# Low value products between the transposes of a head's last run

## The chip, the cores and the metric

The kernel runs on one core of one Trainium2 chip. The metric is the device time of one execution in microseconds (us): before the change the median of 3 runs is 1168.23 us (1168.02 to 1168.42).

## The reference

The program is attention with decay, followed by a feed-forward network (FFN), in float32. Shapes: 8 batches, 8 heads, 576 tokens, 64 dimensions a head; the FFN goes from 512 to 2048 and back for 4608 tokens.

```python
scores = scale * np.matmul(q, k.transpose(0, 1, 3, 2))
decay = cum[:, :, :, None] - cum[:, :, None, :]        # cum: running sum of log f
scores = np.where(causal, -1000000000.0, scores + decay)
attn = np.exp(scores - np.max(scores, axis=-1, keepdims=True))
attn = attn / (np.sum(attn, axis=-1, keepdims=True) + 1e-09)
attn_out = np.matmul(attn, v)
h = x @ w_in                                           # x: the heads side by side
g = np.maximum(h, 0.0) + np.log1p(np.exp(-np.abs(h)))
out = g @ w_out
```

## The kernel before

**Numbers in two halves.** Most products are made of float32 numbers split into a high half in a reduced format (float32r) and a low half, the rest. A product of two such numbers is then a few fast products instead of one slow one. For the values V both halves stand side by side in one stationary tile of 128 columns, `vhl`: columns 0 to 63 are the high half, 64 to 127 the low one. A product with it gives 128 rows of output, and the rows of the two halves are added at the end (`shift` and `put`, L1082 to L1086). The names h and l below are the high and low half of the attention weights.

**A whole head.** 56 of the attention's 70 jobs are whole heads (`whole`, L557); the others, of the first batch, work in plain float32 and are not touched. A whole head goes in these steps. Scores of five query tiles are computed (`stat_tile`, L773), reduced to the row's extreme on VectorE (L804), exponentiated on ScalarE (L832) and scaled by their sums (L862). The weights then lie with queries on partitions, and the value product wants keys there, so they are transposed on TensorE, run by run (`weights`, L872). A run fills one PSUM bank:

- run 0: the small one, 64 queries against the first keys, and the last 64 keys
- run 1: keys 0 to 127, 512 queries, four transposes
- run 2: keys 128 to 255, 448 queries, four transposes
- run 3, the last: keys 256 to 383 with 320 queries and keys 384 to 511 with 192, five transposes

In `turn` (L924) a run takes a bank and transposes its blocks (L927). `hi_part` and `lo_part` (L939, L943) then split the bank into h and l in SBUF (`ph` and `pl`, three buffers each). On the profile's rows the tile of a bank of transposes is `b`, its operands are the weights `p` (stationary) and a constant (`ident`, or `halves`, which also exchanges two halves of 64) as the moving operand of 128 columns.

`output` (L1046) makes the value products of a group of queries in one bank, tile `o`. Group 0 has the first 64 queries, group 1 the other 512. For each key chunk it multiplies `vhl` with h and then with l, over as many moving columns as there are queries: in group 1 these are 512 and 512 for the first chunk, a single one of 64 for the small run, then 448 and 448, 320 and 320, 192 and 192 (L1060).

**The order of the work.** The order on every engine is written down before anything runs. `Plan` (L52) holds operations with an estimated cost, what they come after, and the buffers that they take and give; `run` (L106) always emits the operation that can start earliest by its estimates. Costs are those of `on_pe`, `on_turn` (0.109 us a transpose) and their like (L158 to L188). Operations that need a bank of the tag `att` (four banks, shared by scores, transposes and value products) take it in the order in which they were added, but for scores, which may go ahead where a bank is to spare. On the chip each engine works through its own list in order and waits for the others by semaphores.

A head's runs and outputs are added among the scores of the next head (L1549 to L1562): runs 0 to 2, the output of group 0, run 3, and later the output of group 1. Between these units, parts of the FFN are added, a share of what is ready (`run_ffn`, L1482). So TensorE's list alternates between attention and groups of six FFN products (`up_part`, L1176, with tile `h` at L1210; `products`, L1290, with tile `acc` at L1295). The FFN's work goes on after the last head.

Of the kernel before, what the change touches and what calls it, by code (L numbers as in the profile page):

```python
# [157 lines left out]
def on_pe(n, times=1, m=128):  # L158

    return On("PE", times * (max(n * 0.000444, m * 0.00092) + 0.002))  # L160
# [7 lines left out]
def on_turn(n):  # L168

    return On("PE", 0.109 * n)  # L170
# [49 lines left out]
def tile_decay_attention_softplus_ffn(  # L220
# [51 lines left out]
    def bank(tag, name):  # L272
        return psum.tile([P, 512], F32, tag=tag, name=name, bufs=BUFS[tag])
# [334 lines left out]
    def attention(job):  # L608
# [26 lines left out]
        n = f"{number}"  # L635
# [236 lines left out]
        def weights(bi):  # L872
            spans, w = [], 0
            for key, lo, hi, vi, vc in banks[bi]:
                spans.append((key, lo, hi, (vi, vc), w))
                w += hi - lo


            small = spans[0][:3] == (0, 0, 64)
            blocks, need = [], []  # L880
            for ti, (q0, n_q, k0, pi, po) in enumerate(tiles):
                for key, lo, hi, _, at in spans if small else reversed(spans):
                    if q0 < hi and q0 + n_q > lo and k0 <= key:

                        second = q0 < lo and ti < nt - 1
                        at += q0 - lo + (64 if second else 0)
                        c = po + key - k0
                        if small:  # L890

                            x = pt[pi][:, c : c + 64]
                            one = halves
                            if key == 0:

                                x, one = x[0:68], ident[0:68, 0:68]
                            blocks.append((x, key // 8, one))
                        else:
                            one = halves if second else ident
                            blocks.append((pt[pi][:, c : c + P], at, one))  # L900
                        need += st["norm"][ti]
            box = {}
            sums = job["sums"].get(bi, []) if plain else []
            if sums:
                st["one", bi] = box, w
                need.append(st["over"])
                at1 = w
                w += sum(x[3] for x in sums)

            spread_ = []  # L910
            for ta, tb, *_ in sums:

                def spread(e, ta=ta, tb=tb):
                    one = box["one"] = buf("one", [P, P], f"one{n}_{bi}")
                    x = rs[:, ta : tb + 1]
                    x = bass.AP(x.tensor, x.offset, [x.ap[0], [tb - ta, 2], [0, 64]])
                    copy(e, one.rearrange("p (a b) -> p a b", a=2), x)

                if ta != tb:
                    on = [on_dve(P, True, bias=COPY_BIAS), on_act(P), On("POOL", 0.3)]  # L920
                    spread_.append(add(on, spread, after=[st["over"]], takes=("one",)))
            need += spread_

            def turn(e):  # L924
                box["ps"] = bank("att", f"b{n}_{bi}")
                for x, at, one in blocks:
                    e.transpose(box["ps"][0 : x.shape[1], at : at + one.shape[1]], x, one)  # L927
                for ta, tb, at, _ in sums:
                    one = rs[:, ta : ta + 1].to_broadcast([P, P]) if ta == tb else box["one"]
                    e.transpose(box["ps"][:, at1 + at : at1 + at + P], one, ident)  # L930

            def keep(e):
                box["p"] = buf(tag, [P, 512], f"p{n}_{bi}", F32R)[:, 0:w].bitcast(F32)
                copy(e, box["p"], box["ps"][:, 0:w])

            more, size = ("64", P) if small else ("", 512)
            rows = 64 if small else P

            def hi_part(e):  # L939
                box["h"] = buf("ph" + more, [P, size], f"ph{n}_{bi}", F32R)[:, 0:w]  # L940
                copy(e, box["h"][0:rows], box["ps"][0:rows, 0:w])

            def lo_part(e):  # L943
                if small:
                    h = box["h"]
                    e.tensor_sub(h[64:P], box["ps"][0:64, 0:w], h[0:64].bitcast(F32))
                    return
                box["l"] = buf("pl", [P, size], f"pl{n}_{bi}", F32R)[:, 0:w]
                e.tensor_sub(box["l"], box["ps"][:, 0:w], box["h"].bitcast(F32))  # L949

            need = list(dict.fromkeys(need)) + halves_set
            m = add(on_turn(len(blocks) - 0.48 * small + len(sums)), turn, after=need, takes=("att",))
            for _ in spread_:
                give("one", [m])
            st.setdefault("turned", []).append(m)
            if bi == len(banks) - 1:
                give("p", st["turned"])
                if plain:
                    give("stat", st["turned"])
            on = [on_act(w, psum=True), on_dve(w)]  # L960
            if plain:
                tag = tags[bi] = ("ph", "pl")[count["p"] % 2]
                count["p"] += 1
                ready = [add(on, keep, after=[m], takes=(tag,))]
                give("att", ready)
            else:
                hp = add(on, hi_part, after=[m], takes=("ph" + more,))
                ready = [hp, add(on_dve(w), lo_part, after=[hp], takes=() if small else ("pl",))]
                give("att", ready[1:])
            for key, lo, hi, vc, at in spans:  # L970
                parts.append((lo, hi, bi, vc, at, box, ready, small))
# [74 lines left out]
        def output(gi):  # L1046
            g0, g1, h, tok = groups[gi]
            g, j = h // 2, h % 2
            todo = sorted(
                (p for p in parts if p[0] < g1 and p[1] > g0), key=lambda p: (max(p[0], g0) > g0, p[2])  # L1050
            )
            box, last = {}, []
            for i, (lo, hi, bi, vc, at, pbox, ready, small) in enumerate(todo):
                a, z = max(lo, g0), min(hi, g1)

                def values(e, i=i, a=a, z=z, vc=vc, o=at + a - lo, pbox=pbox, xs="h" if small else "hl"):
                    if i == 0:
                        box["ps"] = bank("att", f"o{n}_{gi}")
                    for x in xs:
                        e.matmul(  # L1060
                            box["ps"][:, a - g0 : z - g0], st["vhl"][:, vc[1], :],
                            pbox[x][:, o : o + z - a],
                            start=i == 0 and x == "h", stop=i == len(todo) - 1 and x == xs[-1],
                        )

                on = on_pe(z - a, len("h" if small else "hl"))
                op = add(
                    on, values, after=ready + last + st["V"],
                    takes=("att",) if i == 0 else (),
                )  # L1070
                last = [op]
                used[bi].append(op)
            st.setdefault("ends", []).extend(last)
            w = g1 - g0


            def to():
                if b not in x_of:
                    x_of[b] = buf("x32", [P, NCC, S], f"x32_{b}")
                return x_of[b][64 * j : 64 * j + 64, g, tok : tok + w]  # L1080

            def shift(e):  # L1082
                copy(e, to(), box["ps"][64 - 64 * j : 128 - 64 * j, 0:w])

            def put(e):
                e.tensor_add(to(), box["ps"][64 * j : 64 * j + 64, 0:w], to())  # L1086

            needs = last + x_taken.get(b, [])
            takes = () if b in x_taken else ("x32",)
            c = add(on_act(w, psum=True), shift, after=needs, takes=takes)  # L1090
            d = add(on_dve(w), put, after=[c])
            x_taken.setdefault(b, [c])
            puts = [d]
            wrote.setdefault(b, []).append((tok, tok + w, d))
            give("att", puts)
            if gi == len(groups) - 1:
                give("T", st["scores"])
                give("vhl", st["ends"])
                for bi, ops in used.items():
                    if banks[bi][0][:3] == (0, 0, 64):  # L1100
                        give("ph64", ops)
                    else:
                        give("ph", ops)
                        give("pl", ops)
# [523 lines left out]
```

## Time and profile before

| | |
|---|---|
| median of 3 runs | 1168.23 us |
| the profiled execution | 1169.16 us |
| its span, first to last instruction | 1167.4 us |
| TensorE products, busy | 1153.1 us (99%) |
| TensorE weight loads, busy | 958.0 us (82%) |
| VectorE, ScalarE, GpSimd, busy | 799.1, 834.1, 146.1 us |
| granted TensorE clock | 1.00 |

In the rows, PE stands for the products of TensorE and PEld for the loads of its stationary operand, which run beside products; DVE is VectorE, ACT ScalarE and POOL GpSimd. A row of a group names line, engine, operation, output and inputs, the stationary operand's rows and columns (128*64 has 64 columns), the shape of the moving operand, and the count; behind the first bar stand busy time in us and the mean of one in ns, behind the second the idle time before them. A row of the timeline has start and covered time in us, and neighbours of the same kind are merged with a count. Products overlap in their pipeline: one takes far longer from its start to its end than from its start to that of the next.

### The profile page before, as it was taken

The page shows a single profiled execution, that of the slowest core. Times are in us where ns is not written, and L with a number is a line of the kernel's source. Part 1 is how long each engine was busy: PE and PEld are TensorE (multiplying, and loading weights), DVE is VectorE, ACT ScalarE, POOL GpSimd, SP SyncE. Part 2 cuts the span into 40 slices and gives each one's busy share as a digit, 9 for nine tenths or more (in the row PEclk, how much of TensorE's full clock was granted, in tenths as well). Part 3 has the DMA queues.
Part 4 walks back from the last instruction along what each step waited for, and adds up shares of the span by engine and source line. Part 5 has one row for each costly group of instructions (what it writes and reads, how often), then busy time and mean ns, then how long its engine had stood idle before and what let it go on. Part 6 is the DMA issues. An engine that isn't in the chain of part 4 may idle for free.

```text
span 1167.4 us, 19457 instructions
## 1 busy us (share of the span) xinstructions
PE 1153.1 (99%) x6236; PEld 958.0 (82%) x6236; DVE 799.1 (68%) x1986; ACT 834.1 (71%) x1987; POOL 146.1 (13%) x158
## 2 busy tenths in 40 slices
PE   8999999999999999999999999999999999999998
PEld 6776788888888888888888888888888888888887
DVE  7889999877776778667877777677866772223322
ACT  6887788978867877678767786787867873444543
POOL 3424221100111101011011001110011100000000
PEclk9999999999999999999999999999999999999999
DMA  8867776555666546656566557654666433211211
GB/s 240 245 211 212 193 187 164 144 153 164 160 195 183 155 133 199 180 156 170 152 173 185 161 152 202 175 153 141 188 169 185 121 110 124 75 54 37 90 55 37
DMA packets 118758, 180.36 MB, mean 155 GB/s; under 512 B 20784, under 2 KB 78416, under 8 KB 118656
## 3 DMA queue, kind: packets, MB, share of 16 engines
q1 hardware_dynamic: 118488, 178.97, 53.7%
q8 instruction: 50, 0.82, 0.3%
q14 instruction: 52, 0.43, 0.1%
q10 hardware_dynamic: 168, 0.15, 0.0%
HBM read 109.98 MB, written 35.95 MB: 125 GB/s over the span
## 4 chain that ended last, share of the span: by engine, by line
PE 85%; DVE 8%; DMA 3%; ACT 2%; issue 1%; SPq 0%; POOL 0%; DVEq 0%; ACTq 0%; POOLq 0%
PE acc L1295 30%; PE h L1210 30%; PE b L927 7%; PE o L1060 6%; PE s L800 3%; PE s L799 3%; DMA T<-T 2%; PE h L1191 1%; DVE s L804 1%; PE s L794 1%; PE acc L1314 1%; ACT p L832 1%; DMA wl<-wil_d 1%; DVE xl L1162 1%; DVE pl L949 1%
## 5 line engine op out<-in xcount | busy, mean ns | idle before, releaser
L1210 PE MATMUL h<-xh,wih 128*128 128x512 f32 (+1 forms) x576 | 230.4, 403 | 0.0
L832 ACT ACTIVATE p<-s,negm 128x288 f32<-128x288 f32 (+7 forms) x384 | 183.6, 481 | 57.2 <-DVE negm L804 52.4
L1210 PE MATMUL h<-xl,wih 128*128 128x512 f32 (+1 forms) x576 | 216.6, 379 | 0.0
L804 DVE CUSTOM_DVE_ANT_0 s<-s,cmask 128x288 f32<-128x288 f32 (+6 forms) x320 | 137.9, 440 | 88.5 <-PE s L800 83.4
L862 POOL TENSOR_SCALAR p<-p,rsum 128x448 f32<-128x448 f32 (+4 forms) x89 | 98.8, 1119 | 744.1 <-DVE rsum L846 390.0
L1257 DVE SCALAR_TENSOR_TENSOR h<-h,e 128x512 f32<-128x512 f32 x136 | 95.8, 705 | 130.5 <-ACT e L1249 129.4
L1243 ACT ACTIVATE e<-h 128x512 f32<-128x512 f32 x144 | 85.9, 597 | 118.2 <-PE h L1210 117.1
L1295 PE MATMUL acc<-woh_dt_float32r,gh 128*128 128x512 f32 x376 | 152.8, 406 | 0.0
L1210 PE MATMUL h<-xh,wl 128*128 128x512 f32 (+1 forms) x576 | 148.8, 380 | 0.0
L1295 PE MATMUL acc<-woh_dt_float32r,gl 128*128 128x512 f32 x376 | 147.2, 391 | 0.0
L1295 PE MATMUL acc<-wol_dt_float32r,gh 128*128 128x512 f32 x376 | 147.0, 391 | 0.0
L949 DVE TENSOR_TENSOR pl<-b,ph 128x512 fp32r<-128x512 f32 x168 | 111.1, 666 | 32.2 <-ACT ph L216 28.9
L216 ACT CAST ph<-b 128x512 fp32r<-128x512 f32 (+2 forms) x178 | 85.3, 483 | 58.2 <-PE b L927 52.6
L1210 PEld LDWEIGHTS h<-xh,wl 128*128 128x128 f32 x576 | 104.8, 188 | 21.6
L927 PE MATMUL b<-ident,p 128*128 128x128 f32 (+1 forms) x728 | 118.8, 269 | 2.5 <-ACT p L832 1.2
L1265 DVE TENSOR_TENSOR gl<-h,gh 128x512 fp32r<-128x512 f32 x136 | 93.6, 688 | 40.4 <-ACT gh L216 39.9
L1210 PEld LDWEIGHTS h<-xh,wih 128*128 128x128 f32 x576 | 108.7, 189 | 15.2 <-issue 0.2
L1210 PEld LDWEIGHTS h<-xl,wih 128*128 128x128 f32 x576 | 108.9, 189 | 14.4 <-DVE xl L1162 0.2
L927 PEld LDWEIGHTS b<-ident,p 128*128 128x128 f32 (+1 forms) x728 | 86.6, 138 | 18.3 <-ACT p L832 3.9
L216 ACT CAST gh<-h 128x512 fp32r<-128x512 f32 x114 | 67.0, 588 | 46.9 <-DVE h L1257 43.3
L799 PE MATMUL s<-T 128*64 128x64 f32 x336 | 98.0, 303 | 0.9 <-ACT p L832 0.6
L800 PE MATMUL s<-T 68*64 68x64 f32 x336 | 97.7, 295 | 0.0
(166 smaller groups left out, 2218.9 us busy)
## 6 DMA issues: line engine op xcount, KB each, us to landing
wl<-wil_d SPq DMA_DIRECT2D x72, 512.0 KB
T<-T SPq DMA_DIRECT2D x224, 144.0 KB
raw<-in_qkT SPq DMA_DIRECT2D x112, 144.0 KB
g_d<-gh SPq DMA_DIRECT2D x84, 128.0 KB
g_d<-gl SPq DMA_DIRECT2D x84, 128.0 KB
vr<-in_vR SPq DMA_DIRECT2D x64, 160.0 KB
out<-ob SPq DMA_DIRECT2D x35, 256.0 KB
sto<-in_w_out SPq DMA_DIRECT2D x11, 512.0 KB
```

Of the source, the lines that this page charges most:

```text
L216: (e.tensor_copy if hasattr(e, "tensor_copy") else e.copy)(out, in_)
L799: e.matmul(o, qA[:, q0:end], kA[:, a:z], start=True, stop=False)
L800: e.matmul(o, qB[0:ST, q0:end], kB[0:ST, a:z], start=False, stop=True)
L804: e.tensor_tensor_reduce(out=box["o"], in0=box["o"], in1=cmask[0:n_q, right - w : right], scale=-0.125, scalar=m0 if i else 3.0e38, op0=AL ...
L832: e.activation(o, box["o"], AF.Exp, bias=m1, scale=-1.0, accum_out=acc)
L862: e.tensor_scalar(a, a, f_, None, ALU.mult)
L927: e.transpose(box["ps"][0 : x.shape[1], at : at + one.shape[1]], x, one)
L949: e.tensor_sub(box["l"], box["ps"][:, 0:w], box["h"].bitcast(F32))
L1210: e.matmul(o, l, r, start=m == 0, stop=m == 11)
L1257: e.scalar_tensor_tensor(h, h, 0.0, box["e"], ALU.max, ALU.add)
L1265: e.tensor_sub(box["l"], box["t"], box["h"].bitcast(F32))
L1295: e.matmul(st["acc", tt], l, r[fc], start=first and m == 0, stop=last and m == 2,)
```

## The change

The value products of runs 1 and 2 for group 1 leave `output` and go into the turn of run 3. This turn now takes two banks at once, `b` for its transposes and `o` for the output, and comes after both halves of runs 1 and 2 and after V. It first makes the two products of h (512 and 448 moving columns, 128 stationary ones). Then it makes the five transposes, and behind each of the first four stands half of a low product: l over 256, 256, 224 and 224 moving columns, with the high half of V alone as the stationary operand, 64 columns. The product of the two low halves, which the kernel before adds to rows 64 to 127, is thereby left out for these two chunks. `output` of group 1 goes on in the same bank with the small run, and with the two chunks of run 3. Runs 1 and 2 give back their buffers after the turn.

The plan's cost of the turn changes: 0.054 us are taken off for each of the four low halves, and the products are added.

```diff
+            mixed = [] if plain or bi < len(banks) - 1 else [x for x in parts if not x[7]]
+            g0 = groups[-1][0]
+
             def turn(e):
                 box["ps"] = bank("att", f"b{n}_{bi}")
+                more = []
+                if mixed:
+                    o = st["o"] = bank("att", f"o{n}_{len(groups) - 1}")
+                    for i, (lo, hi, _, vc, at, pbox, *_) in enumerate(mixed):
+                        a, z = lo - g0, hi - g0
+                        v = st["vhl"][:, vc[1], :]
+                        e.matmul(o[:, a:z], v, pbox["h"][:, at : at + z - a], start=i == 0, stop=False)
+                        w2 = (z - a) // 2
+                        more += [(a + c, w2, v[:, 0:D], pbox["l"][:, at + c : at + c + w2]) for c in (0, w2)]
                 for x, at, one in blocks:
                     e.transpose(box["ps"][0 : x.shape[1], at : at + one.shape[1]], x, one)
+                    if more:
+                        a, w2, v, p_ = more.pop(0)
+                        e.matmul(o[0:D, a : a + w2], v, p_, start=False, stop=False)
...
-            m = add(on_turn(len(blocks) - 0.48 * small + len(sums)), turn, after=need, takes=("att",))
+            on, takes = on_turn(len(blocks) - 0.48 * small + len(sums)), ("att",)
+            if mixed:
+                w2s = [hi - lo for lo, hi, *_ in mixed]
+                cost = on.cost - 2 * len(w2s) * 0.054 + sum(on_pe(w).cost + 2 * on_pe(w // 2).cost for w in w2s)
+                on, takes = On("PE", cost), ("att", "att")
+                need += [r for x in mixed for r in x[6]] + st["V"]
+            m = add(on, turn, after=list(dict.fromkeys(need)), takes=takes)
+            if mixed:
+                st["mixed"] = [m], [x[2] for x in mixed]
+                for x in mixed:
+                    used[x[2]].append(m)
...
-            box, last = {}, []
+            box, last, mixed = {}, [], []
+            if gi == len(groups) - 1:
+                mixed, done = st["mixed"]
+                last = mixed
+                todo = [x for x in todo if x[2] not in done]
...
-                        box["ps"] = bank("att", f"o{n}_{gi}")
+                        box["ps"] = st.pop("o", None) or bank("att", f"o{n}_{gi}")
...
-                            start=i == 0 and x == "h", stop=i == len(todo) - 1 and x == xs[-1],
+                            start=not mixed and i == 0 and x == "h",
+                            stop=i == len(todo) - 1 and x == xs[-1],
...
-                    takes=("att",) if i == 0 else (),
+                    takes=("att",) if i == 0 and not mixed else (),
```

## The prediction

> **What bounds the kernel now.** I read the page's busy times and chain first, then busy time by stage, then the groups by shape and the single instructions of one head.
>
> ```profile
> span 1167.4 us, 19457 instructions
> PE 1153.1 (99%) x6236; PEld 958.0 (82%) x6236; DVE 799.1 (68%) x1986; ACT 834.1 (71%) x1987; POOL 146.1 (13%) x158
> PE 85%; DVE 8%; DMA 3%; ACT 2%; issue 1%; SPq 0%; POOL 0%; DVEq 0%; ACTq 0%; POOLq 0%
> ```
> ```profile
> core 0: us, PE busy (x) PEld busy (x) DVE busy (x) ACT busy (x) POOL busy (x), PEclk, DMA share, GB/s
> ...
> 120.00:250.00 130.00, 126.59 (x789) 106.62 (x788) 115.58 (x313) 110.45 (x290) 24.65 (x20) 1.00 0.64 170
> ...
> 400.00:550.00 150.00, 150.00 (x801) 127.05 (x800) 112.38 (x280) 114.64 (x281) 17.46 (x16) 1.00 0.59 167
> ...
> 970.00:1167.40 197.40, 193.61 (x860) 160.19 (x858) 53.45 (x78) 83.88 (x139) 0.00 (x0) 1.00 0.20 64
> ```
>
> TensorE is never idle from 400 to 550 us (150.00 of 150.00) at the full granted clock, while VectorE and ScalarE work three quarters of it. The whole heads of the edit lie mostly in stages like this, and what one of them saves or costs TensorE goes straight into the end. Only from 120 to 250 us does it idle, for 3.4 us, and there VectorE is busy 89% (115.58 of 130). From 970 us on GpSimd and VectorE have little left: this is the FFN alone, which the edit doesn't touch. Busy time can't say how well TensorE is used, since rows overlap, so the working goes from start to start.
>
> **The change part by part.** It moves two high products (512 and 448 columns) and their low products in front of and between the five transposes of the head's last run, cuts each low product in two and gives it 64 stationary columns. The high products keep their shape and length. What is left is one question: what does a transpose cost when a low product follows it? The order of work before:
>
> ```profile
> 714.22 0.39 PE L1295 MATMUL acc<-woh_dt_float32r,gl_0b 128*128 128x512 f32 x1
> 714.45 0.38 PE L927 MATMUL b<-halves,p 128*128 128x128 f32 x2
> 714.67 0.49 PE L927 MATMUL b<-ident,p 128*128 128x128 f32 x3
> 714.91 0.38 PE L799 MATMUL s<-T 128*128 128x288 f32 x1
> 715.54 0.40 PE L1060 MATMUL o<-ph,vhl 128*128 128x512 f32 x1
> 715.77 0.40 PE L1060 MATMUL o<-pl,vhl 128*128 128x512 f32 x1
> 716.01 0.48 PE L1060 MATMUL o<-ph,vhl 128*128 128x64 f32 x2
> 716.32 0.37 PE L1060 MATMUL o<-pl,vhl 128*128 128x448 f32 x1
> 716.53 0.39 PE L1295 MATMUL acc<-woh_dt_float32r,gh_0b 128*128 128x512 f32 x1
> ```
>
> Five transposes begin 0.11 us apart (714.45 to 714.67 for two). The 512 low product holds TensorE 0.24 (715.77 to 716.01), the 448 one 0.21 (716.32 to 716.53). What do the 0.11 consist of? If it were the weight load, a short load for the low product would release the transpose's second half; if it were the 128 moving columns, nothing is to be had. Durations by shape, and weight loads:
>
> ```profile
> L927 PE MATMUL b<-ident,p 128*128 128x128 f32 x672 | 107.2, 273 | 2.3 <-ACT p L832 1.2 <-DVE p L216 0.5 <-DVE x L1024 0.3
> L927 PE MATMUL b<-ident,p 68*64 68x68 f32 x56 | 12.4, 222 | 0.2 <-POOL p L862 0.2
> L1210 PE MATMUL h<-xh,wl 128*128 128x512 f32 x512 | 138.5, 392 | 0.0
> L1210 PE MATMUL h<-xh,wl 128*128 128x256 f32 x64 | 10.2, 282 | 0.0
> L927 PEld LDWEIGHTS b<-halves,p 128*128 128x128 f32 x176 | 22.7, 142 | 8.2 <-issue 2.2 <-ACT p L832 0.2
> L1060 PEld LDWEIGHTS o<-pl,vhl 128*128 128x128 f32 x224 | 42.4, 189 | 2.2 <-issue 0.2 <-DVE pl L949 0.2
> L799 PEld LDWEIGHTS s<-T 128*64 128x64 f32 x56 | 7.5, 134 | 3.6 <-PE acc L1295 0.5 <-PE h L1210 0.4 <-PE o L1060 0.4
> ```
>
> From 68 to 128 moving columns a transpose grows from 222 to 273 ns, 0.85 ns a column; a product grows from 282 to 392 over 256 columns, 0.43. A transpose thus streams at half the pace of a product, and 128 x 0.85 = 0.109 us, the whole distance. Its load is the short one: 142 ns against 189 for a product with as many stationary columns, about what 64 columns of a product take (134). A place where a transpose had to wait for its load shows the load alone:
>
> ```profile
> 223.59 0.44 PE L927 MATMUL b<-halves,p 128*128 128x128 f32 x2
> 223.58 0.20 PEld L927 LDWEIGHTS b<-halves,p 128*128 128x128 f32 x2
> 223.75 0.36 PEld L927 LDWEIGHTS b<-ident,p 128*128 128x128 f32 x3
> ```
>
> The two loads cover 0.20 with 0.142 for one, so the second began 0.06 after the first; the three behind, in steady work, begin (0.36 - 0.14) / 2 = 0.11 apart. A load of 0.06 can't hold a row of transposes at 0.11. I take the transpose to be bound by its own stream, and so as 0.11 also in front of a low product. No row has a transpose before 64 stationary columns: the bounds are 0.06 (what such a load needs, the next fence) and 0.12 (0.11 and the 0.01 to which starts are read).
>
> The Trainium skill (TensorE: Matmul & The Clock Gate, LDWEIGHTS) gives a load as columns over 1.2 GHz, an estimate of 107 ns for 128 columns and 53 for 64, and its Terms call the transpose mode four times faster for FP32. By that the 0.11 is a load, and the change gains as in the first rival. This trace disagrees, with 0.06 for the load and 0.85 ns a column for the stream.
>
> The low halves, from rows where nothing waits:
>
> ```profile
> 719.55 0.39 PE L1295 MATMUL acc<-woh_dt_float32r,gl_1b 128*128 128x512 f32 x1
> 719.78 0.19 PE L799 MATMUL s<-T 128*64 128x64 f32 x1
> 719.78 0.13 PEld L800 LDWEIGHTS s<-T 68*64 68x64 f32 x1
> 719.84 0.19 PEld L799 LDWEIGHTS s<-T 128*128 128x128 f32 x1
> 191.91 0.52 PE L1210 MATMUL h<-xh,wl 128*128 128x256 f32 x3
> 718.17 0.25 PE L1060 MATMUL o<-ph,vhl 128*128 128x192 f32 x1
> 718.26 0.28 PE L1060 MATMUL o<-pl,vhl 128*128 128x192 f32 x1
> ```
>
> Three products of 256 columns cover 0.52, so they begin (0.52 - 0.28) / 2 = 0.12 apart; 192 columns take 0.09, so 224 about 0.105 (an estimate between the two). Two and two make 0.45, against 0.23 (a 512 one in steady work, 719.55 to 719.78) and 0.21 uncut: +0.01 a head. The fewer stationary columns save nothing, as a load of 0.06 (719.78 to 719.84) or 0.11 is hidden behind either neighbour. Then eight new borders between transposes and products. From a product to a transpose the trace has 0.23 (714.22 to 714.45), no more than between products; I take 0.01 for all eight, with 0 and 0.08 (0.01 each) as ends. The last transpose still exposes a full load of whatever follows, as before. Sum: +0.02 a head, between +0.01 and +0.09; with 56 heads (x56 in the rows) +1.1 us, between +0.6 and +5.0.
>
> **The new wait.** The last run now waits for both halves of the two earlier runs, V, and two free banks at once, where it waited for its scaled weights and one bank.
>
> ```profile
> 713.79 0.62 DVE L949 TENSOR_TENSOR pl<-b,ph 128x448 fp32r<-128x448 f32 x1
> 702.61 0.62 DVE L949 TENSOR_TENSOR pl<-b,ph 128x448 fp32r<-128x448 f32 x1
> 702.56 0.58 PE b L927 x5
> 703.14 0.70 PE acc L1295 x3
> 706.16 4.29 PE acc L1295 x18
> ```
>
> Here rows of VectorE stand before three of the chain of waits. In the head at 714 the low half of the second run ends at 714.41, 0.04 before the transposes begin: nothing to wait for. In the head at 702 it ends at 703.23, about 0.7 after the transposes began (702.56 in the chain). There the three FFN products behind them (0.70) can go first, and 18 follow at 706: the order is planned anew with this dependency, and FFN work is the cover. Without it each such head would stall some 0.7. Queued behind the turn in TensorE's order are FFN products; ScalarE and VectorE wait for its bank to cast the last run, and the remaining five output products for these. The output's bank is held longer from its first product, while the high and low buffers of the first two runs come free sooner. Between 120 and 250 us, with little cover, I add 0.3 (a tenth of the 3.4 idle; ends 0 and 3.4). No DMA is issued by an edited step, and no queue of SP or POOL is passed.
>
> Total against the profiled execution's 1169.16 us: +1.4, 1170.6. That execution lies 0.9 above the median of the runs shown, 1168.23, so the forecast for the median is 1169.6.
>
> **The rivals.** *Loads bound the transposes after all* (0.17): then four of the five cost 0.06 in place of 0.11, a gain of 0.20 - 0.02 = 0.18 a head, 10.1 us, 1158.1. For it speaks that 0.11 is also what 128 stationary columns of a product need when exposed (the two from 716.01 are a product of 64 moving columns and one of 448: 0.31 to the next start, less 0.21, is 0.10); a serial load and stream of a transpose, 0.06 and 0.05, would look like 0.11 as well. Against it stand the two paces per column.
>
> *Each border costs* (0.17): eight turnarounds between the half-pace and the full-pace stream, 0.01 each, with the split 0.09 a head, 5.0 us, 1173.2. It decides from 0.042 a head (2.34 us over 56), about 4 ns a border. Against it stands the 0.23 from product to transpose; the way back is hidden in the trace behind an exposed load, so it is not excluded. An extreme of it: the Trainium skill (TensorEngine Tiling (Array Packing), Key Properties) says that a change of tiling mode drains the engine. Were 64 columns such a mode, a drain of some 0.16 (273 - 109 ns) at each border would make 1240; the score product with 64 columns begins 0.23 after a 512 one, undrained, so I leave that 0.01 of the 0.17.
>
> *The wait shows* (0.08): the early heads stall twice as long, +3.4 us and +1.1, 1172.7; the steady stages don't, by their cover.
>
> That the change doesn't stand where it says can't be: all of it is emitted by one step.
>
> **How the numbers follow.** The forecast has 0.58: 1169.6, by itself 1166.5 to 1173, as a new order of everything may move a few idle stretches either way by a us or two. The range reaches through the two slower cases to 1174.5, and down to 1160 into the neighbourhood of the gain, most of which is left out. Two measurements of this kernel tell about 0.2%, 2.3 us, from nothing. Of the forecast about 0.28 of its weight lies above that, 0.03 below: slower 0.58 x 0.28 + 0.21 = 0.37, faster 0.02 + 0.17 = 0.19, same 0.44.
>
> **What would show it.** In the last run, transposes and low products in turn: from one transpose to the next 0.23 (forecast), 0.18 (loads), 0.25 (borders). A product's row right behind a transpose begins early (the score product at 714.91), so only the distance between transposes counts. TensorE's waits on the low halves should stay below 1 us in the steady stages. A time under 1163 would make the step on the stream wrong; one over 1173 the borders or the wait.

## The result

The changed kernel takes 1174.26 us, the median of 4 runs (1173.53 to 1175.20), against 1168.12 us (1166.45 to 1168.42) for the kernel before. The ratio is 1.0056, with a 95% interval of 1.0039 to 1.0073: it is slower by about 6.1 us. The time lies inside the predicted range, near its upper end, 4.7 us above the forecast of 1169.6. The forecast gave the largest chance, 0.44, to a change too small to tell, and 0.37 to a slower kernel. In the experiments below, one execution with the first eight heads (4029.58 us), one with the wait alone (6553.84 us) and one of the kernel before (1615.70 us) were far slower than the rest; the ratios leave them out, while the medians count them, which raises the first two by 0.7 and 0.4 us.

The page of the changed kernel, profiled in an execution of 1173.53 us:

```profile
span 1171.8 us, 19730 instructions
PE 1155.6 (99%) x6348; PEld 964.7 (82%) x6348; DVE 794.0 (68%) x1991; ACT 823.4 (70%) x1989; POOL 139.1 (12%) x151
```

TensorE's share of busy time says nothing new. The stages do. Busy time by stage, first of the changed kernel, then two of the same stages before:

```profile
core 0: us, PE busy (x) PEld busy (x) DVE busy (x) ACT busy (x) POOL busy (x), PEclk, DMA share, GB/s
...
222.00:236.00 14.00, 10.37 (x50) 8.53 (x49) 10.90 (x30) 9.32 (x25) 3.28 (x2) 0.76 0.39 99
...
300.00:970.00 670.00, 669.46 (x3652) 568.87 (x3651) 485.34 (x1227) 495.64 (x1250) 70.31 (x63) 1.00 0.58 165
```
```profile
222.00:236.00 14.00, 13.83 (x76) 11.56 (x75) 11.80 (x32) 11.77 (x32) 1.52 (x1) 1.00 0.40 97
...
300.00:970.00 670.00, 669.07 (x3572) 565.84 (x3571) 492.40 (x1223) 502.44 (x1231) 71.25 (x68) 1.00 0.58 165
```

In the long steady stage TensorE idles 0.54 of 670 us after (670 - 669.46) and 0.93 before: no stall has appeared there. In the 14 us from 222 it idles 3.63 in place of 0.17. From 120 to 222 it idles no more than before (2.75 against 3.24 by the same view), so the extra idle time of the early stage is in this one hole. The granted clock in the hole, 1.00 before, is 0.76. It is 0.50 where it is lowest (230 to 235 us), so this is 0.24 x 14 / 0.5 = 6.7 us of half clock.

**How late the heads are.** Every whole head has one transpose with 68 rows. Its place in the timeline, for the 8th, the 15th and the 47th whole head, before and then after:

```profile
209.32 0.22 PE L927 MATMUL b<-ident,p 68*64 68x68 f32 x1
...
314.64 0.22 PE L927 MATMUL b<-ident,p 68*64 68x68 f32 x1
...
824.00 0.22 PE L927 MATMUL b<-ident,p 68*64 68x68 f32 x1
```
```profile
212.24 0.22 PE L939 MATMUL b<-ident,p 68*64 68x68 f32 x1
...
318.76 0.22 PE L939 MATMUL b<-ident,p 68*64 68x68 f32 x1
...
829.37 0.22 PE L939 MATMUL b<-ident,p 68*64 68x68 f32 x1
```

At the 8th whole head the changed kernel is 2.9 us late (212.24 - 209.32), at the 15th 4.1, at the 47th 5.4. Most of the loss is there before 319 us. The 32 heads between add 1.25 us, 0.04 a head. One pair of traces tells this to about 0.02 a head: the kernel with only the first twelve heads changed (below) takes 510.03 us for these 32, which it builds as before, against 509.36.

**A steady turn.** The timeline of TensorE in one turn of the changed kernel:

```profile
719.75 0.60 PE L935 MATMUL o<-ph,vhl 128*128 128x512 f32 x2
720.19 0.27 PE L939 MATMUL b<-halves,p 128*128 128x128 f32 x1
720.22 0.36 PE L942 MATMUL o<-pl,vhl 128*64 128x256 f32 x1
720.42 0.27 PE L939 MATMUL b<-halves,p 128*128 128x128 f32 x1
720.45 0.36 PE L942 MATMUL o<-pl,vhl 128*64 128x256 f32 x1
720.65 0.27 PE L939 MATMUL b<-ident,p 128*128 128x128 f32 x1
...
720.86 0.27 PE L939 MATMUL b<-ident,p 128*128 128x128 f32 x1
...
721.08 0.27 PE L939 MATMUL b<-ident,p 128*128 128x128 f32 x1
```

From one transpose to the next it is 0.23 with a half of 256 columns between (720.19, 720.42, 720.65) and 0.21 to 0.22 with one of 224 (720.65, 720.86, 721.08). That is 0.11 for the transpose and 0.12 or 0.10 for the low half, the same as each takes in a row of its kind. The row of a low half begins 0.03 behind its transpose (720.22), but the next transpose is not early, so only the distance between transposes counts.

**The stall.** The same kernel's timeline of TensorE around its longest idle time:

```profile
221.18 0.39 PE L1325 MATMUL acc<-woh_dt_float32r,gl 128*128 128x512 f32 x1
...
225.59 0.27 PE L1089 MATMUL o<-ph,vhl 128*128 128x64 f32 x1
227.46 0.37 PE L799 MATMUL s<-T 128*128 128x288 f32 x1 [1.60 <-DVE pl L964]
...
228.76 0.42 PE L939 MATMUL b<-halves,p 128*128 128x128 f32 x1
...
229.18 0.42 PE L939 MATMUL b<-ident,p 128*128 128x128 f32 x1
...
231.62 0.32 PE L799 MATMUL s<-T 128*64 128x64 f32 x1 [1.17 <-ACT p L832]
231.86 0.77 PE L1240 MATMUL h<-xh,wih 128*128 128x512 f32 x1
```

The last FFN product ahead of the hole starts at 221.18, and the next at 231.86: for 10 us TensorE has nothing but attention. In this time it waits 0.75 and 1.17 for ScalarE's exponentials, and 1.60 for VectorE's low half, with no FFN product between. From 228.76 a transpose takes 0.42 in place of 0.27 and the distance through a low half is 0.42 (228.76 to 229.18) in place of 0.23: the half clock. The product at 231.86 is the first of a block of 512 columns. Why is there no FFN work earlier? It comes in blocks, a block needs the outputs of the heads before it, and the first whole heads have beside them the last products of the plain first blocks and then only one block of 256 columns. Of this block's products with the second FFN matrix one of three kinds, from 120 to 222 us, before and then after:

```profile
L1295 PE MATMUL acc<-woh_dt_float32r,gh 128*128 128x512 f32 x25 | 10.0, 401 | 0.0
```
```profile
L1325 PE MATMUL acc<-woh_dt_float32r,gh 128*128 128x512 f32 x32 | 13.1, 409 | 0.0
```

By 222 us the changed kernel has done 32 of the kind, which is the whole block (16 slices of the hidden width times two tiles of 128 tokens), where the kernel before shows 25. The next block, of 512 columns, waits for the eighth whole head. In the kernel before, the rows show that head's last addition to the FFN's input `x`, the last split of that input into halves, the last product of the old block that is ready, the split that delays its last eighth (`gl`), and the first product after it:

```profile
217.35 0.69 DVE L1086 TENSOR_TENSOR x<-o,x 64x512 f32<-64x512 f32 x1
221.81 1.21 DVE L1162 TENSOR_TENSOR xl<-x,xh 128x1024 fp32r<-128x1024 f32 x1
222.92 0.40 PE L1295 MATMUL acc<-woh_dt_float32r,gl 128*128 128x512 f32 x1
...
226.21 0.68 DVE L1265 TENSOR_TENSOR gl<-h,gh 128x512 fp32r<-128x512 f32 x1
...
229.40 0.41 PE L1295 MATMUL acc<-woh_dt_float32r,gh 128*128 128x512 f32 x1
```

And after:

```profile
223.53 0.69 DVE L1116 TENSOR_TENSOR x<-o,x 64x512 f32<-64x512 f32 x1
...
229.88 1.22 DVE L1192 TENSOR_TENSOR xl<-x,xh 128x1024 fp32r<-128x1024 f32 x1
```

Before, the last split of `x` ends at 223.02 and the ready part of the narrow block ends with the product at 222.92: the supply just reaches. The block's last eighth is still held up behind VectorE then, and comes after 229.40 beside the new block, whose first product starts at 224.48. After, the eighth head ends 6.2 us later (223.53 against 217.35) and the split of `x` ends at 231.10, with the old block used up to the last product.

### The profile page after: what moved, and what is told of

Same layout as the page of the kernel before. It is cut to its first block, busy times and chain, and to the rows that moved or that the text cites. A ratio compares the mean times of both kernels' runs of the same rounds, so it can differ in the third digit from the quotient of the medians.

```text
span 1171.8 us, 19730 instructions
## 1 busy us (share of the span) xinstructions
PE 1155.6 (99%) x6348; PEld 964.7 (82%) x6348; DVE 794.0 (68%) x1991; ACT 823.4 (70%) x1989; POOL 139.1 (12%) x151
## 4 chain that ended last, share of the span: by engine, by line
PE 91%; DVE 5%; ACT 2%; issue 1%; POOL 0%; DVEq 0%; ACTq 0%; POOLq 0%
PE h L1240 32%; PE acc L1325 31%; PE b L939 8%; PE s L799 4%; PE s L800 4%; PE o L1089 3%; PE o L942 2%; PE o L935 2%; PE h L1221 2%; PE acc L1344 2%; PE s L794 1%; DVE s L804 1%; ACT p L832 1%; PE o L1025 0%; PE warm L1553 0%
## 5 line engine op out<-in xcount | busy, mean ns | idle before, releaser
L862 POOL TENSOR_SCALAR p<-p,rsum 64x64 f32<-64x64 f32 (+4 forms) x82 | 92.1, 1130 | 755.8 <-DVE rsum L846 434.1
L216 ACT CAST ph<-b 128x512 fp32r<-128x512 f32 (+2 forms) x164 | 80.3, 492 | 84.4 <-PE b L939 77.8
L939 PE MATMUL b<-ident,p 128*128 128x128 f32 (+1 forms) x728 | 130.7, 270 | 2.8 <-ACT p L832 1.9
L939 PEld LDWEIGHTS b<-ident,p 128*128 128x128 f32 (+1 forms) x728 | 90.8, 139 | 18.7 <-ACT p L832 4.9
L799 PE MATMUL s<-T 128*64 128x64 f32 x336 | 101.5, 313 | 3.2 <-DVE pl L964 1.8
```

Of the source, the lines that this page charges most:

```text
L216: (e.tensor_copy if hasattr(e, "tensor_copy") else e.copy)(out, in_)
L799: e.matmul(o, qA[:, q0:end], kA[:, a:z], start=True, stop=False)
L862: e.tensor_scalar(a, a, f_, None, ALU.mult)
```

## The experiments

The differences in us below are the ratio times the median of the kernel before in the same set of runs (1168.68, 1169.21 and 1168.80 us).

### Which heads lose the time

The same change for a part of the heads only. The whole heads have the numbers 14 to 69.

```diff
-            mixed = [] if plain or bi < len(banks) - 1 else [x for x in parts if not x[7]]
+            mixed = [] if plain or bi < len(banks) - 1 or not (number >= 26) else [x for x in parts if not x[7]]
...
-            if gi == len(groups) - 1:
+            if gi == len(groups) - 1 and "mixed" in st:
```

**From the 13th whole head on (44 heads).**

> The change is made only in whole heads from the 13th on (head number 26 and more, 44 heads); the first 12 are built as in the kernel before. Theory of the stage (the loss of the changed kernel arises between 120 and 250 us, where the early heads have little FFN work to hide their waits and the clock falls; a steady head costs +0.02 us): 44 x 0.02 = +0.9 us over the kernel before, and no idle stretch over 1 us after 200 us. Theory of the price per head (all of the loss is spread evenly, 6.1 / 56 = 0.11 a head): +4.8 us.

**The first 12 whole heads only:** the same line with `number < 26`.

> The change is made only in the first 12 whole heads (numbers 14 to 25); the other 44 are built as in the kernel before. Theory of the stage: nearly the whole loss, +4 to +6 us, with an idle TensorE around 223 to 232 us and a granted clock of 0.5 behind it. Theory of the price per head: 12 x 0.11 = +1.3 us.

**The first 8 whole heads only:** with `number < 22`.

> The change is made only in the first 8 whole heads (numbers 14 to 21), those whose outputs the first wide FFN block reads; the 48 others are built as before. If the loss is that these heads end later while the FFN work that covers them is used up, so that TensorE stands idle before the wide block can begin: +3 to +6 us, with an idle TensorE between 222 and 236 us. If the four heads after them, which have no such work beside them, make it: within 1 us of the kernel before.

The late heads alone: 1168.86 us, ratio 1.0002 (0.9993 to 1.0011). The first twelve alone: 1174.35 us, 1.0042 (1.0028 to 1.0055), +4.9 us. The first eight alone: 1172.67 us, 1.0032 (1.0011 to 1.0053), +3.7 us. Busy time from 222 to 236 us in the three, in this order:

```profile
222.00:236.00 14.00, 13.71 (x76) 11.87 (x77) 11.47 (x32) 11.75 (x30) 1.51 (x1) 1.00 0.45 103
```
```profile
222.00:236.00 14.00, 10.37 (x51) 8.49 (x50) 11.13 (x31) 9.75 (x26) 3.85 (x2) 0.76 0.34 86
```
```profile
222.00:236.00 14.00, 11.54 (x62) 9.60 (x61) 12.91 (x38) 10.78 (x32) 2.90 (x2) 0.88 0.36 91
```

With the late heads alone TensorE idles 0.29 there and nothing is lost. With the first twelve the hole is that of the whole change (3.63), and so is the clock (0.76). With the first eight it idles 2.46. So the loss comes from the early heads, and by the medians most of it from the first eight, those that the first block of 512 columns waits for (+1.3 to +6.2 by the interval, against +3.3 to +6.4 for the twelve). For the 44 late heads the change is worth 0.2 us, and by the interval -0.8 to +1.3 us, which is -0.02 to +0.03 a head.

### The wait and the banks without the moved products

**The wait alone.** The kernel before, with the last run waiting in the plan for both halves of runs 1 and 2 and for V.

```diff
+            if not plain and bi == len(banks) - 1:
+                need = list(dict.fromkeys(need + [r for x in parts if not x[7] for r in x[6]] + st["V"]))
```

> The kernel before, with one thing added: in the plan the turn of the last run comes after both halves of runs 1 and 2 and after V, as in the changed kernel. It takes one bank, and all products stand where they stood. If the wait is what makes the early heads late: +3 to +6 us, all of it before 250 us. If the two banks or the planner's lower cost do it: within 1 us of the kernel before.

**The wait and the second bank.** The turn also takes the output's bank. The products stay in `output`.

```diff
+                if not plain and bi == len(banks) - 1:
+                    st["o"] = bank("att", f"o{n}_{len(groups) - 1}")
...
+                takes = ("att", "att")
...
-                        box["ps"] = bank("att", f"o{n}_{gi}")
+                        box["ps"] = st.pop("o", None) or bank("att", f"o{n}_{gi}")
...
-                    takes=("att",) if i == 0 else (),
+                    takes=("att",) if i == 0 and gi < len(groups) - 1 else (),
```

> The kernel before, with the wait of the run named wait and also the output's bank of group 1 taken by the turn of the last run, so that the turn needs two free banks at once and the output's bank is held longer; all products stand where they stood. If holding two banks makes the early heads late: +3 to +6 us here and less in wait. If the wait alone does it: both alike. If neither, and the plan's lower cost does it: both within 1 us of the kernel before.

The wait alone: 1171.93 us, 1.0027 (1.0015 to 1.0039), +3.2 us. With the bank: 1174.83 us, 1.0053 (1.0040 to 1.0065), +6.2 us. So the order that the wait and the banks force costs as much as the whole change, with no product moved. But where these two lose it differs from the changed kernel: from 222 to 236 us they idle 0.00 and 0.25, and have no hole. The 8th, 15th and 47th heads with the wait alone:

```profile
209.67 0.23 PE L927 MATMUL b<-ident,p 68*64 68x68 f32 x1
...
314.36 0.22 PE L927 MATMUL b<-ident,p 68*64 68x68 f32 x1
...
825.68 0.22 PE L927 MATMUL b<-ident,p 68*64 68x68 f32 x1
```

The 8th head of the kernel with the bank:

```profile
212.52 0.22 PE L929 MATMUL b<-ident,p 68*64 68x68 f32 x1
```

The first whole head doesn't start at the same time in all traces: 128.84 before, 128.25 with the change, 127.84 with the wait alone, 128.04 with the bank. Counted from it, the 8th head comes after 80.48, 83.99, 81.83 and 84.48 us. So the wait alone makes the early heads some 1.4 us late, and the second bank as well 4.0, against 3.5 in the changed kernel. With the wait alone the 32 steady heads take 511.32 against 509.36, 0.06 a head more: part of its loss lies there, where the expectation had all of it before 250 us. TensorE idles no more in the steady stage (0.76 of 670 us against 0.93), so this part is no stall.

By these single traces the early heads are delayed less by the wait for the low halves than by the two banks taken at once, of the four that scores, transposes and outputs share. A second bank without the wait was not run. The kernel with the bank idles early too, though in another place, 5.03 us in the 80 from 120, against 2.71 before:

```profile
120.00:200.00 80.00, 74.97 (x481) 61.97 (x480) 74.17 (x198) 66.57 (x175) 14.58 (x12) 1.00 0.64 180
```

Each edit makes a new plan of the whole order, so these two kernels bound what the wait and the banks can cost; they don't split the changed kernel's 6.1 us into shares.

### The interleaving, the 64 columns and the planner's cost

**Not interleaved.** The low products stay whole, with 64 stationary columns, ahead of the five transposes, in the same turn and plan.

```diff
-                        w2 = (z - a) // 2
-                        more += [(a + c, w2, v[:, 0:D], pbox["l"][:, at + c : at + c + w2]) for c in (0, w2)]
+                        e.matmul(o[0:D, a:z], v[:, 0:D], pbox["l"][:, at : at + z - a], start=False, stop=False)
```

> The changed kernel with its plan untouched, but nothing between the transposes: the turn makes the high product and then the whole low product (64 stationary columns) of each of the two chunks, and then its five transposes in a row. If a transpose is bound by its own stream, the interleaving is worth nothing: within 1.5 us of the changed kernel (1174), and the transposes 0.11 apart. If it is bound by the load of what follows, taking the low halves out of the row loses 0.20 us a head: 11 us more, 1185.

**All 128 columns.** The halves stand between the transposes, with both halves of V stationary.

```diff
-                        more += [(a + c, w2, v[:, 0:D], pbox["l"][:, at + c : at + c + w2]) for c in (0, w2)]
+                        more += [(a + c, w2, v, pbox["l"][:, at + c : at + c + w2]) for c in (0, w2)]
...
-                        e.matmul(o[0:D, a : a + w2], v, p_, start=False, stop=False)
+                        e.matmul(o[:, a : a + w2], v, p_, start=False, stop=False)
```

> The changed kernel with 128 stationary columns in the four low halves in place of 64, all else alike (the product of the two low halves is made again). If a transpose streams for 0.11, a load of 0.11 is just hidden behind it: the distance from transpose to transpose stays 0.23 and 0.21, and the time within 1.5 us of the changed kernel. If the load of 64 columns is what lets the low product start early, the distance grows by 0.05 each, 11 us in all.

**The planner's cost without the 0.054 taken off.**

```diff
-                cost = on.cost - 2 * len(w2s) * 0.054 + sum(on_pe(w).cost + 2 * on_pe(w // 2).cost for w in w2s)
+                cost = on.cost + sum(on_pe(w).cost + 2 * on_pe(w // 2).cost for w in w2s)
```

> The changed kernel with one number of the plan changed: the 0.054 us that it takes off for each low half are not taken off, so that the plan knows the turn at 1.45 us, near the 1.41 that the trace shows, and not at 1.24. If the wrong cost makes the plan run out of FFN work around 223 us: no idle stretch over 1 us there, and +0.5 to +3 us over the kernel before. If the wait and the two banks do it by themselves, as the runs wait and banks had +3 and +6 with right costs: +3 to +6 us again.

Not interleaved: 1174.91 us, 1.0057 (1.0037 to 1.0077), as the change itself. All 128 columns: 1173.20 us, 1.0036 (1.0024 to 1.0048). With the other cost: 1175.91 us, 1.0049 (1.0036 to 1.0062). The timeline of a turn without interleaving, and one with 128 columns:

```profile
720.86 0.39 PE L935 MATMUL o<-ph,vhl 128*128 128x512 f32 x1
...
721.73 0.38 PE L938 MATMUL b<-halves,p 128*128 128x128 f32 x2
721.95 0.49 PE L938 MATMUL b<-ident,p 128*128 128x128 f32 x3
```
```profile
719.75 0.27 PE L939 MATMUL b<-halves,p 128*128 128x128 f32 x1
719.78 0.36 PE L942 MATMUL o<-pl,vhl 128*128 128x256 f32 x1
719.98 0.27 PE L939 MATMUL b<-halves,p 128*128 128x128 f32 x1
```

Without interleaving the turn lasts from 720.86 to 721.95 and three transposes more, 1.09 + 3 x 0.11 = 1.42. Interleaved it lasted from 719.75 to 721.08 and one transpose, 1.33 + 0.11 = 1.44. The transposes don't care what stands between them. With 128 stationary columns the next transpose comes after 0.23 as well (719.75 to 719.98), so the short load saves nothing here.

The planner's wrong estimate isn't the cause either. With the other cost the hole is still there, this time at full clock:

```profile
222.00:236.00 14.00, 10.40 (x63) 8.47 (x62) 13.14 (x37) 9.82 (x29) 3.19 (x2) 1.00 0.44 109
```

TensorE idles 3.60 there, and the kernel is 5.7 us slower all the same. All five executions of this kernel had a mean granted clock of 0.999 or 1.000. So the half clock isn't needed for the loss.

### What a transpose waits for

Three rows of 16 transposes each at the start of the kernel, behind six more warming products: 128 stationary and 128 moving columns, then 68 rows and 68 moving columns under 128 stationary ones, then 64 stationary and 128 moving ones. The work is added, so the kernel's own time says nothing.

```diff
+        for _ in range(6):
+            e.matmul(o[:, 0:MW], cmask[:, 0:P], cmask, start=True, stop=True)
+        for _ in range(16):
+            e.transpose(o[:, 0:P], cmask[:, 0:P], ident)
+        for _ in range(16):
+            e.transpose(o[:, 0:68], cmask[0:68, 0:P], ident[0:68, 0:68])
+        for _ in range(16):
+            e.transpose(o[0:64, 0:P], cmask[:, 0:64], ident)
```

> The kernel before with three rows of 16 transposes each at its start, behind six more warming products: 128 stationary and 128 moving columns; 128 stationary and 68 moving; 64 stationary and 128 moving. Nothing waits between them. Bound by the stream: 0.109, 0.059 and 0.109 us apart. Bound by the load of the next: 0.109, 0.109 and 0.06.

The groups by shape, busy time and mean of one in ns behind the first bar:

```profile
L1527 PE MATMUL warm<-ident,cmask 128*128 128x128 f32 x16 | 1.9, 272 | 0.0
L1529 PE MATMUL warm<-ident,cmask 68*128 68x68 f32 x16 | 1.2, 226 | 0.0
L1531 PE MATMUL warm<-ident,cmask 128*64 128x128 f32 x16 | 1.9, 273 | 0.0
```

The granted clock is 1.00 in all three. By the timeline sixteen in a row cover 1.91 us, of which the last one takes 0.27: they begin (1.91 - 0.27) / 15 = 0.109 apart. With half the stationary columns nothing changes. With 68 rows and moving columns in place of 128 the sixteen cover 1.16 and begin (1.16 - 0.23) / 15 = 0.062 apart. Were the 0.109 the load of 128 stationary columns, the third row would be faster and the second would not.

### A short load where a load is exposed

The kernel before with its plan as it was. Only `output` is edited: the low product of run 2 comes right behind the small run's product of 64 columns, all low products have 64 stationary columns, and the two chunks of the last run change places. It leaves out the product of the two low halves in all low products that it narrows.

```diff
+            todo[-2:] = todo[-2:][::-1]
...
-                def values(e, i=i, a=a, z=z, vc=vc, o=at + a - lo, pbox=pbox, xs="h" if small else "hl"):
+                def values(e, i=i, a=a, z=z, vc=vc, o=at + a - lo, pbox=pbox, xs="h" if small else "lh" if bi == 2 or vc[1] == 2 else "hl"):
...
+                        m = D if x == "l" else 2 * D
...
-                            box["ps"][:, a - g0 : z - g0], st["vhl"][:, vc[1], :],
+                            box["ps"][0:m, a - g0 : z - g0], st["vhl"][:, vc[1], 0:m],
```

> The kernel before, its plan all but untouched: the low products of the output have 64 stationary columns (the product of the two low halves is left out), all stay in output, and their order makes use of it: the second chunk's low product stands right behind the small run's product of 64 moving columns, and the last two chunks change places, 192 high, 192 low, 320 low, 320 high. If a short load pays only behind a stream shorter than a load (0.03 behind 64 columns, 0.09 behind 192): 0.05 + 0.02 + 0.02 = 0.09 a head, 5 us less than the kernel before, 1164. If fewer stationary columns pay nowhere: within 1.5 us of it.

1165.32 us, ratio 0.9967 (0.9945 to 0.9989): 3.9 us faster than the kernel before (1.3 to 6.4 by the interval), where I expected 5. The timeline of its first chunks:

```profile
712.67 0.19 PE L1062 MATMUL o<-ph,vhl 128*128 128x64 f32 x1
712.70 0.40 PE L1062 MATMUL o<-pl,vhl 128*64 128x448 f32 x1
712.94 0.36 PE L1062 MATMUL o<-ph,vhl 128*128 128x448 f32 x1
```

From 712.67 to 712.94 stand the product of 64 columns and one of 448. The latter takes 0.21, so the former holds TensorE 0.06. In the kernel before, the product of 64 and the one of 448 behind it took 0.31 (716.01 to 716.32), 0.10 for the product of 64. There the next load had 128 columns, here it has 64. That the load ahead of the second product sets the 0.10 and the 0.06 fits both, and is not tested apart from the new order. Over the steady heads, 15th to 47th, the gain is about 0.10 a head (506.15 us against 509.36); what the exchange of the last chunks has of it was not separated.

## Why the prediction was wrong

**What bounds the kernel: right.** The steady stage is TensorE's, and what a head gains there shows in the end (the last experiment).

**The transpose is bound by its own stream: right.** The forecast from one transpose to the next was 0.23; measured were 0.23 and 0.21 to 0.22. Rows of transposes alone confirm it: 0.109 whatever the stationary columns. The rival that loads bound the transposes (0.18 between transposes, 1158.1 us) falls with this, and with the two kernels in which neither interleaving nor the 64 columns are worth anything. By the load time of the Trainium skill (TensorE: Matmul & The Clock Gate, LDWEIGHTS), columns over 1.2 GHz, a row of transposes that loads bound would take half of the 0.109 with half the stationary columns; the trace has 0.109 for both.

Two readings beside this step were wrong, without changing the sum. A row with a transpose ahead of 64 stationary columns does stand in the trace of before (220.72 and 220.78, 0.06 apart, with 68 moving columns in the first). And the way back from a transpose to a product is not hidden: the last of the three transposes of 714.67 begins at 714.89 and the second product behind it at 715.13. These 0.24 are the transpose's 0.11 and the 0.13 of 288 columns, with nothing left for a border or an exposed load.

**The +0.02 a head: right in the turn, and not excluded by the end.** The late heads alone measure -0.02 to +0.03 a head. The rival of the borders, 0.09 a head, would have cost 44 x 0.09 = 4.0 us there, where 1.3 is the upper end. It came near the measured time with 1173.2, by luck and for a wrong reason: a time between 1173 and 1174 could not tell it from a stall, the experiment by heads could.

**The step that failed is the new wait: "FFN work is the cover", and "Between 120 and 250 us, with little cover, I add 0.3".** I read the cover at 702 and 714 us, where FFN products are in plenty, and took a tenth of the early stage's idle time for a place where they are not. In its place the runs showed +4.9 us (3.3 to 6.4) from the first twelve heads alone, with 3.63 us of idle time in one hole. What I missed is that the cover has a stock and a delivery date. The stock is one block of 256 columns. Even before the change, what was ready of it ended just in time (a product at 222.92, the next block's input split at 223.02). The delivery depends on the eighth head, which the turn itself makes later: by the kernel with the bank the second bank does most of this, where the forecast's bound was built on low halves that come late. So, as the traces read, the heads' delay counts twice: the stock is spent beside the waiting heads, and the next block comes later by the sum of the delays, 6.2 us at the end of the eighth. How close the supply was could be told without a new measurement: both rows stand in the trace of before. That the time still fell into the predicted range is owed to the room that the two slower rivals had in it, not to the 0.3.

The third rival, *the wait shows*, had the right place, and I gave it 0.08. Its price, 3.4 us for the early heads, is to be set against 4.9 (interval 3.3 to 6.4) in the kernel with the first twelve heads changed. So the rival that I had named as the least likely is the nearest to what happened. But it had the early heads stall twice as long, each at its wait, and from 120 to 222 us they stall no longer than before; that its 3.4 is close to the 3.46 us by which the hole idles more is luck.

**The TensorE clock** was no term of the sum. It fell to half for 6.7 us in the hole of the changed kernel, and it does so in some of the kernels that have such a hole and not in others: 0.76 over the 14 us with the whole change and with the first twelve heads, 1.00 with the other cost. Busy time around it in the changed kernel:

```profile
228.00:235.00 7.00, 5.83 (x24) 5.01 (x23) 4.87 (x12) 4.05 (x10) 1.97 (x1) 0.55 0.24 55
```

The mean granted clock of all four executions of the changed kernel is 0.994 to 0.997 (0.003 of 1172 us is 7 us of half clock). It is 0.999 or 1.000 in all five with the other cost, which are nearly as slow: 1.0049 against 1.0056. How much the fall adds can be estimated from kernels whose executions differ in it with one and the same order. With the first eight heads, the four executions at 0.999 took 1169.74 to 1171.94 us, the three at 0.996 and 0.997 took 1173.53 to 1175.42: 3.1 more on average, for about 5.5 us of half clock. Three at 0.998 took 1170.91 to 1173.40, and one at 0.991 took 1179.28. With 128 columns it was 1173.20 at 0.999 (the profiled execution, whose hole is at full clock) and 1174.16 and 1174.98 at 0.996: 1.4 more for about 7. By these the 6.7 us of half clock would go with some 1 to 4 us. That is an estimate from few executions, with the clock known to 0.001; what the fall costs is not shown.

**What stays open:** how the loss divides into the wait, the second bank, the moved products and the clock. The hole stands in the traces of all kernels whose early heads have the products moved, and not in the two that have the wait and the banks alone, so the second bank's part in the hole is argued from how late it makes the eighth head. Open is also why the wait alone costs the steady heads 0.06 each without a stall, while the whole change, which has the same wait, costs them 0.04 by one pair of traces, and -0.02 to +0.03 when the early heads are left as they were.

## What to carry to other kernels

Price a new wait in the stage with the least cover, not in the stage where most of the work is. Ask there how much filler is left, when the next filler becomes ready, and whether that date hangs on the chain that the wait lengthens. If it does, the delay is paid once more when the filler runs out.

In these runs fewer stationary columns paid behind a product of 64 moving columns (0.06 in place of 0.10), and not behind transposes of 128, which take their 0.11 anyway. Find such a place in the distances between starts before moving anything, and take it without a new dependency if it can be had.

## What the hardware showed that was not expected

**Half clock without a long idle gap.** The longest idle time before the fall at about 228.7 us was 1.60 us. In a stretch of 3.4 us that ends 0.3 us into the fall (0.04 x 3.4 / 0.5) TensorE was busy for 1.80, by the same view of the changed kernel, and for 1.73 in the 3.4 us ahead of 228.70:

```profile
225.60:229.00 3.40, 1.80 (x11) 1.61 (x12) 3.40 (x8) 2.10 (x5) 0.00 (x0) 0.96 0.40 104
```

The Trainium skill (TensorE: Matmul & The Clock Gate, What's actually happening) puts the half clock behind an idle window of about 3.4 us. The size agrees, 0.50 of full speed from 230 to 235 us, and the 6.7 us are near two such windows. But here a stretch of that length that was about half busy was followed by the fall, so it is not only complete idleness that brings it. Nor does a hole of this kind always bring it: the kernel with 128 columns idles 3.67 us in the same 14 us of its profiled execution, at full clock.

**A row that begins early.** A product behind a transpose, or behind a product of 64 columns, has its start 0.03 us behind the start of its forerunner (720.19 and 720.22, 712.67 and 712.70), though the one ahead holds TensorE for 0.06 to 0.11. Only the start of the row after next tells what the pair cost.
